# An attention and two-FFN kernel: 13 instead of 20 transfers per attention unit on SyncE's queue, x stored by GpSimd, the attention's order planned anew, six weight halves decoded after it

## The chip, the cores and the metric

The kernel runs on one core of one Trainium2 chip. The metric is the device time of one execution in microseconds. Before the change three runs gave 1263.87, 1264.07 and 1265.71 us (median 1264.07).

## What is computed

```python
B, H, S, D = 4, 8, 576, 64                                  # q, k, v: [B, H, S, D]
scores = q @ k.T / sqrt(D), causal;  a = softmax(scores);  local = a @ v
q_p = where(q > 0, q, exp(q) - 1) + 1
mem_out = (q_p @ M_prev) / (q_p . z_prev + 1e-6)            # M_prev [B,H,D,D], z_prev [B,H,D]
g = sigmoid(beta)                                            # one per head
x = g * mem_out + (1 - g) * local                            # -> [B*S = 2304, H*D = 512]
h = x @ w_in;  x = act(h) @ w_out                            # twice: 512 -> 2048 -> 512, own weights and act
```

Everything is float32; the weights come as float64, and the kernel decodes them itself from pairs of 32-bit words.

## The kernel before

**Attention, then the two FFN layers.** The attention is cut into 16 units u = 0 to 15, each one batch and one pair of heads. Layer 1 then runs over 18 chunks of 256 tokens in pairs, in two halves of the hidden width; layer 2 follows.

**One unit.** SyncE (SP in the rows) loads k, q and v (`load_rows`, three transfers each), for q two more (`qb`, the last 64 rows laid out apart for each head), and M_prev and z_prev (`load_mem`, four). TensorE (PE) transposes k and q into a PSUM tile (`k1`, `q1`); ScalarE (ACT) and VectorE (DVE) split them into two parts (`k2`, `k3`, `q2`, `q3`) and form q_p (`f1` to `f3`). PE makes the scores in four pieces (s0, s1, s2, s3; L478, L471); DVE masks and takes the row's extreme (L493), ACT the exponential (L497). PE transposes the exponentials (`ta`, `tb0` to `tb3`, L411), ACT moves them to SBUF (L506), and PE multiplies with v into the PSUM tile O: `v0` (L521), `v1`, `v2` (L528 to L531). `norms` (L537) puts q_p . z into O as well. DVE turns the sums into factors (`l1` to `l4`, L542 to L547), PE transposes them (`l5`, L548), ACT copies them out (`l6`, L550), and SP writes them to DRAM (`l7`, L551, r_d) and reads them back, repeated over the partitions, into tile R with three transfers (`l8`, `spread`, L560): two for the first plane of R, which weighs the local part, the third for the second plane. DVE multiplies O into R in two pieces (`weigh`, also x1, L575) and the memory's product (`m1`, L569, in a PSUM tile W) into R's second plane (x2, L578). GpSimd (POOL) adds the planes (x3, L580), and SP stores x (L581).

**What is shared.** There is one PSUM tile O, so `v0` of unit u+1 waits for `weigh` of unit u. There are three PSUM tiles W (W_101 to W_103 in the order's rows) for k1, q1, the scores, the transposes and m1; the tile of m1 comes free at x2. R has two buffers, but the plan gives every unit the same one, so the spread of u+1 also waits until x of u is stored.

**The order.** Every engine runs its instructions in a fixed order, which a planner writes (`Plan.order`): each step has an engine, a length, a priority (10 u + PRIO[key]), what it comes after and the buffers it needs; a lag is added to its end. A step on SP costs 80 to 330 ns per group of transfers, and the spread ends 2.5 us after its cost. The planner takes the step that can start first. The 16 halves of layer 1's first weights (`weight_half`: one 512 KB load into one of three buffers `raw`, two ACT and six DVE instructions each) and the first two token chunks (`first_chunk`) are steps of the same plan.

**Layer 1** starts with its own code order: per step of the hidden width 12 matmuls for h (L697 to L699), ACT and DVE for the activation (L707 to L713), and two steps later 12 matmuls for y (L727 to L729). Instructions of later weights are put between those of DVE (`fill`).

Of the kernel before, what the change touches and what calls it, by code (L numbers as in the profile page):

```python
# [9 lines left out]
F32R = mybir.dt.float32r  # L10
# [29 lines left out]
PRIO = dict(load=-14.0, k=-12.9, q=-8.2, phi=16.4, s0=-2.4, s1=0.8, s2=0.1, s3=0.6, ta=-9.1, tb0=4.7, tb1=4.8, tb2=-10.3, tb3=2.5,  # L40
            v0=8.6, n=34.3, l=7.5, v1=43.2, v2=11.8, m=11.9, x=38.4, w=(2.77, 1.99), c=10.2)
EVACUATE = dict(ta="ACT", tb0="ACT", tb1="ACT", tb2="ACT", tb3="ACT")
ROOMS = dict(W=3, O=1, q=2, k=2, v=2, mem=2, ks=2, qs=2, eq=1, ph=2, st=2, R=2, rt=2, e128=4, e256=4, e384=4, e512=4, e576=2,
# [18 lines left out]
class Plan:  # L62
# [25 lines left out]
    def order(self):  # L88
# [3 lines left out]
        while any(todo.values()):  # L92
            best = None
            for engine, ts in todo.items():
                first, now = None, idle.get(engine, 0.0)
                for t in ts:
                    x = self.ready(t, now)
                    if x is not None and (first is None or x < first[0] - 1e-9):
                        first = x, t
                        if x <= now + 1e-9:  # L100
                            break
# [3 lines left out]
            x, t = best  # L105
# [23 lines left out]
def attn_moe_moe_kernel(ctx, tc, q, k, v, m_prev, z_prev, beta, w1i, w1o, w2i, w2o, out):  # L129
# [71 lines left out]
    def new_e(w, i):  # L201
        x = att_tile(f"e{w}", i, w if w < S else 640)
        if w == S:
# [89 lines left out]
    def fetch_halves(seg, halves):  # L293
# [8 lines left out]
        raws = [load_raw(seg, *h) for h in halves[0:ahead]]  # L302
# [112 lines left out]
    stored = []  # L415

    def attention_unit(u):
# [5 lines left out]
        q, k, v, mem = Room("q"), Room("k"), Room("v"), Room("mem")  # L423
        ks, qs, eq, ph, st, R, O = Room("ks"), Room("qs"), Room("eq"), Room("ph"), Room("st"), Room("R"), Room("O")

        def load_q():
            x, qb = at(q)
            load_rows(q_in, x, u)
            for h in range(2):
                nc.sync.dma_start(out=qb[64 * h:64 * h + 64, h], in_=q_in[b, 2 * p + h, 512:576])  # L430

        def load_mem():
            m, z = at(mem)
            for h in range(2):
# [16 lines left out]
        q1 = add("PE", 670, "q", [ld_q], [t, q], lambda t=t: transposes(at(t), [  # L451
            (128 * j, at(q)[0][:, j].rearrange("p h d -> p (h d)")) for j in range(NKT)] + [
            (S, at(q)[1].rearrange("p h d -> p (h d)"))]), "T")
        q2 = add("ACT", from_psum(704), "q", [q1], [t, qs], lambda t=t: act.activation(
            at(qs)[:, 0], at(t)[:, 0:704], AF.Copy, scale=-0.125))
        q3 = add("DVE", dve(704), "q", [q2], [t, qs], lambda t=t: vec.scalar_tensor_tensor(
            out=at(qs)[:, 1], in0=at(t)[:, 0:704], scalar=-0.125, in1=as_r(at(qs)[:, 0]), op0=ALU.mult, op1=ALU.subtract))

        f1 = add("ACT", from_psum(S), "phi", [q1], [t, eq], lambda t=t: act.activation(at(eq), at(t)[:, 0:S], AF.Exp))
        f2 = add("DVE", 370, "phi", [f1], [eq], lambda: vec.tensor_scalar(  # L460
            out=at(eq), in0=at(eq), scalar1=1.0, scalar2=None, op0=ALU.min))
        f3 = add("DVE", dve(S), "phi", [f2], [t, eq, ph], lambda t=t: vec.scalar_tensor_tensor(
            out=at(ph)[:, 0:S], in0=at(t)[:, 0:S], scalar=0.0, in1=at(eq), op0=ALU.max, op1=ALU.add))
# [566 lines left out]
```

## Time and profile before

| | us |
|---|---|
| median of the three runs | 1264.07 |
| the profiled execution | 1263.82 |
| its span in the profile | 1262.0 |
| first spread of the attention (unit 0) issued at | 41.89 |
| last spread (unit 15) issued at | 451.88 |
| x2 of unit 15 starts at | 467.63 |

The 1.8 us between the span and the execution's own time lie around the program. Times in rows count from the span's start. A spread is found in the rows as three L560 transfers. A chain row gives start, length and what it was; a timeline row start, length, engine, line, operation, and in brackets the idle time ahead of it and what ended that.

### The profile page before, as it was taken

The page shows a single profiled execution, that of the slowest core. Times are in us where ns is not written, and L with a number is a line of the kernel's source. Part 1 is how long each engine was busy: PE and PEld are TensorE (multiplying, and loading weights), DVE is VectorE, ACT ScalarE, POOL GpSimd, SP SyncE. Part 2 cuts the span into 40 slices and gives each one's busy share as a digit, 9 for nine tenths or more (in the row PEclk, how much of TensorE's full clock was granted, in tenths as well). Part 3 has the DMA queues.
Part 4 walks back from the last instruction along what each step waited for, and adds up shares of the span by engine and source line. Part 5 has one row for each costly group of instructions (what it writes and reads, how often), then busy time and mean ns, then how long its engine had stood idle before and what let it go on. Part 6 is the DMA issues. An engine that isn't in the chain of part 4 may idle for free.

```text
span 1262.0 us, 18665 instructions
## 1 busy us (share of the span) xinstructions
PE 1083.3 (86%) x7032; PEld 954.5 (76%) x7032; DVE 770.9 (61%) x1706; ACT 516.4 (41%) x988; POOL 55.1 (4%) x59
## 2 busy tenths in 40 slices
PE   4767566667676559999999999999999999999998
PEld 3655445555454438888898887889999999999998
DVE  3554444545453314465985767669978789866665
ACT  3545433444453303243464233336444436443432
POOL 1000000000000000000000000000000000111121
PEclk9877676767677669999999999999999999999999
DMA  5333234333322112132441535422333311213121
GB/s 141 93 97 100 80 91 119 97 87 81 94 83 62 36 39 67 34 117 67 152 129 38 156 111 153 131 84 68 118 101 101 101 51 41 78 52 101 51 84 51
DMA packets 128858, 111.49 MB, mean 88 GB/s; under 512 B 73552, under 2 KB 108928, under 8 KB 128768
## 3 DMA queue, kind: packets, MB, share of 16 engines
q1 hardware_dynamic: 128480, 110.04, 29.3%
q8 instruction: 55, 0.90, 0.3%
q14 instruction: 35, 0.29, 0.1%
q10 hardware_dynamic: 288, 0.26, 0.1%
HBM read 86.52 MB, written 23.75 MB: 87 GB/s over the span
## 4 chain that ended last, share of the span: by engine, by line
PE 68%; DMA 21%; DVE 5%; SPq 3%; ACT 2%; issue 1%; DVEq 0%; ACTq 0%
DMA R<-r_d 19%; PE A L697 5%; PE A L698 5%; PE A L699 5%; PE A L770 5%; PE A L769 5%; PE A L768 5%; PE W L411 4%; PE y L793 2%; PE y L792 2%; PE y L791 2%; PE y L727 2%; PE y L728 2%; PE y L729 2%; PE W L478 2%; PE A L727 2%
## 5 line engine op out<-in xcount | busy, mean ns | idle before, releaser
L770 PE MATMUL A<-ffn_x,i 128*128 128x256 f32 x576 | 163.1, 283 | 0.0
L769 PE MATMUL A<-ffn_x,i 128*128 128x256 f32 x576 | 163.0, 283 | 0.0
L768 PE MATMUL A<-ffn_x,i 128*128 128x256 f32 x576 | 163.0, 283 | 0.0
L707 ACT ACTIVATE g<-A 128x512 f32<-128x512 f32 (+1 forms) x80 | 44.4, 555 | 258.3 <-PE A L699 258.2
L411 PE MATMUL W<-ident,e 128*128 128x128 f32 x400 | 82.8, 363 | 73.7 <-DVE R L578 51.9
L411 PEld LDWEIGHTS W<-ident,e 128*128 128x128 f32 x400 | 65.6, 195 | 83.3 <-DVE R L578 55.9
L965 ACT ACTIVATE gh<-g 128x896 fp32r<-128x896 f32 x72 | 68.8, 955 | 124.9 <-PE A L792 74.3
L709 DVE SCALAR_TENSOR_TENSOR g<-A,g 128x512 f32<-128x512 f32 (+1 forms) x80 | 50.8, 636 | 105.0 <-ACT g L708 105.0
L770 PEld LDWEIGHTS A<-ffn_x,i 128*128 128x128 f32 x576 | 110.6, 192 | 0.0
L768 PEld LDWEIGHTS A<-ffn_x,i 128*128 128x128 f32 x576 | 110.6, 192 | 0.0
L769 PEld LDWEIGHTS A<-ffn_x,i 128*128 128x128 f32 x576 | 110.6, 192 | 0.0
L944 DVE TENSOR_TENSOR gl<-g,gh 128x896 fp32r<-128x896 f32 x72 | 86.6, 1203 | 33.4 <-ACT gh L965 33.4
L493 DVE CUSTOM_DVE_ANT_0 e<-W,mask 128x128 f32<-128x128 f32 (+2 forms) x144 | 67.7, 517 | 34.5 <-PE W L478 22.6
L497 ACT ACTIVATE e<-e,mx 128x128 f32<-128x128 f32 (+2 forms) x144 | 82.4, 574 | 13.4 <-DVE mx L493 13.3
L506 ACT ACTIVATE pb<-W 128x640 f32<-128x640 f32 (+1 forms) x64 | 42.3, 674 | 98.2 <-PE W L411 97.8
L773 ACT ACTIVATE g<-A 128x512 f32<-128x512 f32 x72 | 42.8, 594 | 89.0 <-PE A L770 86.3
L521 PE MATMUL O<-pa,v 128*64 128x256 f32 (+1 forms) x128 | 22.1, 491 | 64.0 <-DVE R L575 64.0
L575 DVE TENSOR_TENSOR R<-O,R 128x256 f32<-128x256 f32 (+1 forms) x32 | 14.6, 458 | 101.0 <-DMA R<-r_d 98.7
L697 PE MATMUL A<-ffn_x,i 128*128 128x512 f32 (+1 forms) x160 | 60.1, 375 | 14.7 <-DVE R L578 14.7
L521 PEld LDWEIGHTS O<-pa,v 128*64 128x64 f32 x128 | 11.2, 197 | 73.1 <-DVE R L575 67.3
L578 DVE TENSOR_TENSOR R<-W,R 128x576 f32<-128x576 f32 x16 | 12.1, 757 | 82.1 <-DMA R<-r_d 82.1
L816 POOL TENSOR_TENSOR ys<-ys,pp 128x512 f32<-128x512 f32 x16 | 27.1, 1717 | 748.3 <-DVE ys L811 748.3
(210 smaller groups left out, 3119.8 us busy)
## 6 DMA issues: line engine op xcount, KB each, us to landing
raw<-in_moe_w_in_dram SPq DMA_DIRECT2D x32, 512.0 KB
raw<-in_moe_w_out_dram SPq DMA_DIRECT2D x32, 512.0 KB
xf<-y_d SPq DMA_DIRECT2D x18, 512.0 KB
xf<-x_d SPq DMA_DIRECT2D x10, 512.0 KB
R<-r_d SPq DMA_DIRECT2D x16, 288.0 KB
x_d<-R SPq DMA_DIRECT2D x16, 288.0 KB
xf<-yp_d SPq DMA_DIRECT2D x9, 512.0 KB
op_d<-ys SPq DMA_DIRECT2D x18, 256.0 KB
```

Source lines behind the costliest of these rows:

```text
L411: pe.transpose(t[:, c:c + 128], x, ident)
L493: lambda t=t, x=x, w=w, c=512 * h + c, mk=mk, col=col: vec.tensor_tensor_reduce(out=at(x)[:, 0:w], in0=at(t)[:, c:c + w], in1=mk, op0=ALU. ...
L497: lambda x=x, w=w, col=col: act.activation(at(x)[:, 0:w], at(x)[:, 0:w], AF.Exp, bias=at(st)[1][:, col:col + 1], scale=-1.0, accum_out=at( ...
L697: nc.tensor.matmul(hx, wh, xh[:, ct], start=(ct == 0), stop=False)
L698: nc.tensor.matmul(hx, wh, xl[:, ct], start=False, stop=False)
L699: nc.tensor.matmul(hx, wl, xh[:, ct], start=False, stop=(ct == 3))
L709: nc.vector.scalar_tensor_tensor(out=g, in0=hp, scalar=1.0, in1=g, op0=ALU.max, op1=ALU.min)
L768: nc.tensor.matmul(o, wh, xh[:, ct], start=(s == 0 and ct == 0), stop=False)
L769: nc.tensor.matmul(o, wh, xl[:, ct], start=False, stop=False)
L770: nc.tensor.matmul(o, wl, xh[:, ct], start=False, stop=(s == 1 and ct == 3))
L944: nc.vector.tensor_tensor(gl, g[:, 1:8], as_r(gh), ALU.subtract)
L965: nc.scalar.activation(gg[1], gg[0][:, 1:8], AF.Copy)
```

## The change

- The steps of a unit: q is loaded without `qb`, by three transfers; the last 64 rows are laid out apart by two GpSimd copies inside `qs` (`apart`, q4), and `q1`, `q2`, `q3` work on 576 columns instead of 704. q_p is built in its own tile `ph`.
- M_prev and z_prev are loaded once per batch (four transfers for four units) instead of per unit.
- x is stored by a transfer that GpSimd issues. q of unit 0 is loaded from ACT's queue.
- SP's steps now cost 570 ns per transfer (`SEND`) in the plan; the spread's lag stays 2.5 us. The priorities are new. The planner now prefers among ready steps the one with the lowest priority number, plus 1.25 (`STAY`) where PE would change its mode.
- The halves 10 to 15 of the weights are decoded in layer 1, at its steps 0 to 10; the first three of their loads stay in the plan.

```diff
+PRIO = dict(load=-48.26, v=-40.11, mem=-30.82, k=-3.3, q=-1.74, phi=35.91, s0=-19.51, s1=-15.79, ...
+EARLY, STAY = 10, 1.25
...
                 for t in ts:
+                    if first is not None and t.prio > first[2]:
+                        break
                     x = self.ready(t, now)
...
+                    if x > now + 1e-9:
+                        if first is None or x < first[0] - 1e-9:
+                            first = x, t, 1e9
+                    else:
+                        p = t.prio + STAY * (t.mode != mode and engine == "PE")
+                        if first is None or p < first[2]:
+                            first = now, t, p
...
-        def load_q():
-            x, qb = at(q)
-            load_rows(q_in, x, u)
-            for h in range(2):
-                nc.sync.dma_start(out=qb[64 * h:64 * h + 64, h], in_=q_in[b, 2 * p + h, 512:576])
...
+                r = slice(64 * h, 64 * h + 64)
+                nc.sync.dma_start(out=m[r, :, h], in_=m_prev[b, h::2].rearrange("p d e -> d p e"))
+                nc.sync.dma_start(out=z[r, :, h], in_=z_prev[b, h::2].rearrange("p d -> d p"))
+
+        if p == 0:
+            memory_of[b] = mem = Room("mem")
+            memory_of[b] = mem, add("SP", 2 * SEND + 2 * SEND, "mem", (), [mem], load_mem)
...
+        ld_k = add("SP", 3 * SEND, "load", (), [k], lambda: load_rows(k_in, at(k), u))
+        ld_q = add("SP" if u else "ACT", 3 * SEND, "load", (), [q], lambda: load_rows(q_in, at(q), u), lag=2.3)
+        ld_v = add("SP", 3 * SEND, "v", (), [v], lambda: load_rows(v_in, at(v), u))
...
+        def apart():
+            x = at(qs)
+            for h in range(2):
+                r = slice(64 * h, 64 * h + 64)
+                pool.tensor_copy(x[r, :, S + 64 * h:S + 64 * h + 64], x[r, :, 512:S])
+
+        q4 = add("POOL", 600, "q", [q3], [qs], apart)
...
-        l8 = add("SP", 240, "l", [l7], [R], spread, lag=2.5)
+        l8 = add("SP", 3 * SEND, "l", [l7], [R], spread, lag=2.5)
...
-        stored.append(add("SP", 80, "x", [x3], [R], lambda: nc.sync.dma_start(
+        stored.append(add("POOL", 1000, "x", [x3], [R], lambda: pool.dma_start(
             out=x_d[b][128 * p:128 * p + 128], in_=at(R)[:, 0])))
...
+    decoded = [weight_half(n, n // 2, n % 2) for n in range(EARLY)]
...
+    for h in late[0:RAWB]:
+        plan.add("SP", SEND, 10 * B * NP + 99, plan.tasks[-6:] + decoded, [Room("raw")], lambda h=h: first_raws.append(load_raw(0, *h)), lag=3.8)
+    for i, h in enumerate(late):
+        at_step(2 * i + 2, split_half, 0, *h)
+        for _ in range(5):
+            at_step(2 * i, piece, part)
```

PE's order from m1 of unit 9 to l5 of unit 10, before. O_104 is the PSUM tile O; rows of transposes that repeat are left out at "..." (`ident,e` is a transpose of exponentials, `ident,k` k1).

```order
L569 MATMUL W_101<-ph_136,mz_125 128x512
...
L411 MATMUL W_103<-ident,e_158 128x128
...
L521 MATMUL O_104<-pa_144,v_117 64x256 x2
...
L411 MATMUL W_101<-ident,e_162 128x128
...
L537 MATMUL O_104<-zz_122,ph_134 128x2 x5
...
L411 MATMUL W_103<-ident,k_113 128x128 x5
L478 MATMUL W_102<-ks_130,qs_132 128x128 x6
L478 MATMUL W_102<-ks_130,qs_132 128x256 x6
L478 MATMUL W_101<-ks_130,qs_132 128x512 x6
L548 MATMUL O_104<-ident,st_141 128x128
```

The same place with the change (line numbers are 8 to 13 higher).

```order
L582 MATMUL W_103<-ph_133,mz_117 128x512
...
L419 MATMUL W_101<-ident,e_155 128x128
...
L534 MATMUL O_104<-pa_141,v_113 64x256 x2
...
L550 MATMUL O_104<-zz_118,ph_131 128x2 x5
L419 MATMUL W_103<-ident,e_155 128x128
...
L419 MATMUL W_101<-ident,e_159 128x128
...
L491 MATMUL W_102<-ks_126,qs_127 128x128 x6
L491 MATMUL W_102<-ks_126,qs_127 128x256 x6
L561 MATMUL O_104<-ident,st_138 128x128
```

Before, tb3 into W_101, the tile that m1 of unit 9 holds until x2, stands ahead of norms, and k1 and s2 of other units stand ahead of l5. Now norms stands ahead of the first transposes into m1's tile (W_103), and between that point and l5 stand tb1, tb3 and s0 alone.

DVE's order from weigh of unit 9 to l4 of unit 10, before.

```order
L575 TENSOR_TENSOR R_146<-O_104,R_146 128x256
L575 TENSOR_TENSOR R_146<-O_104,R_146 128x320
L617 TENSOR_TENSOR w_1739<-da,dr 128x512
...
L578 TENSOR_TENSOR R_146<-W_101,R_146 128x576
L456 SCALAR_TENSOR_TENSOR qs_132<-W_102,qs_132 128x704
L460 TENSOR_SCALAR eq_133<-eq_133 128x576
L598 TENSOR_SCALAR da<-raw 128x512
L462 SCALAR_TENSOR_TENSOR ph_136<-W_102,eq_133 128x576
...
L544 TENSOR_SCALAR st_141<-O_104 128x10
...
L547 TENSOR_TENSOR st_141<-st_141,gates 128x19
```

With the change.

```order
L588 TENSOR_TENSOR R_143<-O_104,R_143 128x256
L588 TENSOR_TENSOR R_143<-O_104,R_143 128x320
L462 SCALAR_TENSOR_TENSOR qs_127<-W_102,qs_127 128x576
L591 TENSOR_TENSOR R_143<-W_103,R_143 128x576
L473 TENSOR_SCALAR ph_133<-ph_133 128x576
L475 SCALAR_TENSOR_TENSOR ph_133<-W_102,ph_133 128x576
L557 TENSOR_SCALAR st_138<-O_104 128x10
L559 RECIPROCAL st_138<-st_138 128x19
L560 TENSOR_TENSOR st_138<-st_138,gates 128x19
```

q3 has moved ahead of x2, and the decode's instructions (L598 to L617 before) no longer stand between.

SP's order between two spreads with the change: from the spread of unit 4 to that of unit 5.

```order
L573 DMA R_143<-r_d_175 128x1x576
L388 DMA q_105<-in_q_dram 128x4x64 x2
...
L388 DMA v_113<-in_v_dram 128x4x64 x2
...
L400 DMA raw<-x_d_187 128x4x256
L388 DMA k_111<-in_k_dram 128x4x64 x2
...
L286 DMA raw<-in_moe_w_in_dram 128x4x256
L564 DMA r_d_176<-rt_145 19x128
L289 DMA raw<-in_moe_w_out_dram 128x1024
L573 DMA R_143<-r_d_176 128x1x512
```

Here a load of weights stands between r_d and the spread; in units 9 to 14 nothing does, and the store of x is gone from this queue.

## Rows read from the trace of the kernel before

**Rows 1.** The page's head: span and instructions.
```profile
span 1262.0 us, 18665 instructions
```
**Rows 2.** Stretches: length, busy PE, PEld, DVE, ACT, POOL; granted clock, DMA share, GB/s.
```profile
42.00:468.00 426.00, 274.59 (x1759) 213.88 (x1759) 186.93 (x516) 174.87 (x427) 21.52 (x15) 0.71 0.30 82
468.00:520.00 52.00, 51.55 (x218) 42.51 (x219) 21.42 (x33) 15.25 (x29) 1.40 (x1) 0.95 0.20 63
462.00:467.00 5.00, 0.00 (x0) 0.00 (x0) 0.12 (x1) 0.00 (x0) 0.00 (x0) 0.50 0.13 51
```
**Rows 3.** The chain in order of time, spread of unit 8 to unit 9.
```profile
258.57 0.55 SPq L560
...
259.72 15.10 DMA R<-r_d
...
274.91 0.76 DVE R L578
...
275.82 2.37 PE W L411 x10
278.18 1.93 PE O L537 x10
280.11 2.23 PE W L411 x10
282.35 1.58 PE W L478 x7
283.92 0.42 PE O L548
...
284.71 1.60 DMA r_d<-rt
...
286.36 0.54 SPq L560
```
**Rows 4.** SP's timeline: spreads of units 0, 2, 6, 14, 15 and one r_d.
```profile
41.89 3.72 SPq L560 DMA_DIRECT2D R<-r_d  x3
...
89.17 0.26 SPq L551 DMA_DIRECT2D r_d<-rt  x1
93.64 4.92 SPq L560 DMA_DIRECT2D R<-r_d  x3
...
202.95 4.67 SPq L560 DMA_DIRECT2D R<-r_d  x3
...
424.21 3.75 SPq L560 DMA_DIRECT2D R<-r_d  x3
...
451.88 3.66 SPq L560 DMA_DIRECT2D R<-r_d  x3
```
**Rows 5.** DVE's timeline: x2 of unit 0, weigh's end and x2 of 15.
```profile
58.72 0.76 DVE L578 TENSOR_TENSOR R<-W,R 128x576 f32<-128x576 f32 x1 [3.96 <-DMA R<-r_d]
...
461.63 0.49 DVE L575 TENSOR_TENSOR R<-O,R 128x320 f32<-128x320 f32 x1 [1.97 <-DMA R<-r_d]
467.63 0.76 DVE L578 TENSOR_TENSOR R<-W,R 128x576 f32<-128x576 f32 x1 [5.51 <-DMA R<-r_d]
```
**Rows 6.** Timeline of the start: first scores of unit 0, and ACT's first decode.
```profile
14.03 1.30 PE L411 MATMUL W<-ident,k 128*128 128x128 f32 x5 [6.00 <-DMA k<-in_k_dram]
...
17.48 1.65 PE L478 MATMUL W<-ks,qs 64*128 64x128 f32 x12
...
23.98 0.68 ACT L593 ACTIVATE w<-raw 128x512 f32<-128x512 f32 x1 [5.64 <-DMA raw<-in_moe_w_in_dram]
```
**Rows 7.** Timeline at the attention's end: x3, store, and who waits for it.
```profile
468.52 1.40 POOL L580 TENSOR_TENSOR R<-R 128x576 f32<-128x576 f32 x1 [26.24 <-DVE R L578]
...
469.95 0.34 SPq L581 DMA_DIRECT2D x_d<-R  x1
...
472.15 0.69 DVE L713 TENSOR_TENSOR gl<-g,gh 128x512 fp32r<-128x512 f32 x1 [1.94 <-DMA x_d<-R]
```
**Rows 8.** DVE by line, 42 to 468 us: count, busy us, mean ns.
```profile
L617 DVE TENSOR_TENSOR w<-da,dr 128x512 f32<-128x512 f32 x15 | 10.8, 718 | 0.1
```

More of the change, by code (lines that the diff above doesn't have):

```diff
@@ L38 @@
 HALVES = {N1: [82 + 7 * i // 2 for i in range(16)], N1 + 1: [x for x in range(150, 209) if x % 8 in (0, 6)]}
-PRIO = dict(load=-14.0, k=-12.9, q=-8.2, phi=16.4, s0=-2.4, s1=0.8, s2=0.1, s3=0.6, ta=-9.1, tb0=4.7, tb1=4.8, tb2=-10.3, tb3=2.5,
-            v0=8.6, n=34.3, l=7.5, v1=43.2, v2=11.8, m=11.9, x=38.4, w=(2.77, 1.99), c=10.2)
+PRIO = dict(load=-48.26, v=-40.11, mem=-30.82, k=-3.3, q=-1.74, phi=35.91, s0=-19.51, s1=-15.79, s2=6.04, s3=-14.57, ta=-66.58, tb0=-44.92,
+            tb1=-21.43, tb2=-29.5, tb3=-16.11, v0=-23.74, n=-32.83, l=-36.92, v1=6.21, v2=23.96, m=23.51, x=55.42, w=(2.48, 4.3, 19.15), c=1.18)
+EARLY, STAY = 10, 1.25
 EVACUATE = dict(ta="ACT", tb0="ACT", tb1="ACT", tb2="ACT", tb3="ACT")
-ROOMS = dict(W=3, O=1, q=2, k=2, v=2, mem=2, ks=2, qs=2, eq=1, ph=2, st=2, R=2, rt=2, e128=4, e256=4, e384=4, e512=4, e576=2,
+ROOMS = dict(W=3, O=1, q=2, k=2, v=2, mem=2, ks=2, qs=2, ph=2, st=2, R=2, rt=2, e128=4, e256=4, e384=4, e512=4, e576=2,
              pa=2, pb0=1, pb1=1, pb2=1, pb3=1)
@@ L96, in order @@
                 for t in ts:
+                    if first is not None and t.prio > first[2]:
+                        break
                     x = self.ready(t, now)
[L98 to L101, printed above, removed]
+                    if x is None:
+                        continue
+                    if x > now + 1e-9:
[5 more added lines that the diff above has]
+                            first = now, t, p
                 if first is not None and (best is None or first[0] < best[0]):
@@ L301, in fetch_halves @@
             return
-        raws = [load_raw(seg, *h) for h in halves[0:ahead]]
+        raws = [load_raw(seg, *h) for h in halves[0:ahead]] if seg else first_raws
         for k, (f, x) in enumerate(halves):
@@ L376, in load_rows @@
     def load_rows(src, t, u):
+        queue = nc.scalar if u == 0 and src is q_in else nc.sync
         b, p = UNITS[u]
@@ L414, in attn_moe_moe_kernel @@
     WIDTH = (128, 256, 384, 512, S)
-    stored = []
+    stored, memory_of = [], {}
+    SEND = 570
     def attention_unit(u):
@@ L450, in attention_unit @@
         t = Room("W")
[L451 to L463, printed above, removed]
+        q1 = add("PE", 560, "q", [ld_q], [t, q], lambda t=t: transposes(at(t), [
+            (128 * j, at(q)[:, j].rearrange("p h d -> p (h d)")) for j in range(NKT)]), "T")
@@ L483, in attention_unit @@
             t = Room("W")
-            s = add("PE", cost, f"s{n}", [q2, q3, k2, k3], [t, qs, ks], lambda t=t, rows=rows: products(t, rows),
+            s = add("PE", cost, f"s{n}", [q3, k3, q4 if rows == (4,) else None], [t, qs, ks], lambda t=t, rows=rows: products(t, rows),
                     "T" if rows == (4,) else "R")
@@ L606, in high @@
             act.activation(got["o"][:, 0], got["w"], AF.Copy)
-        t = plan.add("SP", 80, prio - 20, (), [raw], load, lag=3.8)
+        t = plan.add("SP", SEND, prio - PRIO["w"][2], (), [raw], load, lag=3.8)
         t1 = plan.add("ACT", 574, prio, [t], [raw, w32], first)
@@ L619, in weight_half @@
         t2 = plan.add("ACT", 536, prio, [t2], [w32], high)
-        plan.add("DVE", 602, prio, [t2], [w32], low)
+        return plan.add("DVE", 602, prio, [t2], [w32], low)
     def first_chunk(i):
@@ L629, in load @@
             load_chunk(i, got["x"])
-        t = plan.add("SP", 80, prio, stored[0:NP], [raw], load, lag=3.8)
+        t = plan.add("SP", SEND, prio, stored[0:NP], [raw], load, lag=3.8)
         t = plan.add("ACT", from_sbuf(1024), prio, [t], [raw], lambda: act.activation(ffn_x[0][:, i], got["x"], AF.Copy))
@@ L981, in attn_moe_moe_kernel @@
         attention_unit(u)
-    for n in range(2 * NSLOT):
-        weight_half(n, n // 2, n % 2)
+    decoded = [weight_half(n, n // 2, n % 2) for n in range(EARLY)]
     for i in range(2):
         first_chunk(i)
+    late = sorted(((n // 2, n % 2) for n in range(EARLY, 2 * NSLOT)), key=lambda h: (h[1], h[0]))
+    first_raws = []
+    part = fetch_halves(0, late)
+    for h in late[0:RAWB]:
[4 more added lines that the diff above has]
+            at_step(2 * i, piece, part)
     engines = {e.engine for e in (nc.tensor, nc.scalar, nc.vector, nc.gpsimd)}
```

47 lines of the change are left out of this document (25 added, 22 removed).

## The prediction

> **What bounds the kernel now.** I read stretches first, then the chain in order of time over one unit, then SP's and DVE's timelines. The span is 1262.0 us [rows 1]; the execution took 1263.8, 1.8 more, and lies 0.3 under the median of 1264.07, so differences are taken from 1263.8 and stand for the median as well. The stretches show that from 42 to 468 us PE is busy 275 of 426 us at a mean granted clock of 0.71, DVE 187 and ACT 175, so no engine is full; from 468 on PE has no gap (51.6 of 52 us) [rows 2]. The attention is therefore bound by a wait, the later layers by PE, and what the change is worth is decided before 468 us.
>
> The wait is seen in one unit [rows 3]. The spread of unit 8 is issued at 258.57, its third transfer lands before x2 at 274.91, x2 ends at 275.67, and the spread of unit 9 is issued at 286.36. So a unit's cycle has two parts: from spread to the end of x2, 17.1 us (17.6 in unit 0, 16.5 in unit 15 with no loads beside it [rows 4, 5]), and from there to the next spread, 10.7 us, which I call the tail. Spread 0 is at 41.89, spread 15 at 451.88: 410.0 us for 15 cycles, 27.3 each [rows 4]. The cycle closes because weigh frees O for v0 of the next unit and x2 frees m1's tile W, on which transposes ahead of l5 wait.
>
> **The spread itself stays.** Its three transfers are unchanged. While only they run, DMA is busy 0.13 of 16 engines, two engines' worth, at 51 GB/s [rows 2]: the 576 KB are limited by themselves, not by the queue's other transfers. I take 17.4 us per unit from spread to x2's end, and 16.5 in units 14 and 15. Taking 7 transfers per unit off SP gives nothing by itself: the chain of rows 3 has SP only for the spread's own issue.
>
> **The tail, step by step.** In rows 3 it is 0.15 us to PE, ten transposes 2.37, norms 1.93, ten more 2.23 (tb1 and k1), scores 1.58, l5 0.42, then 0.37 over l6 to the issue of r_d and 1.65 until the spread: 10.7. In the new order of unit 9 to 10 norms stands ahead of the tile that waits for x2, and weigh is done early enough for it: weigh's second piece starts 9.8 us after the spread in unit 15 and takes 0.5 [rows 4, 5], v0 I put at 1.6 like the scores, tb2 at 1.2 (half of 2.37), norms at 1.93, together 15.0 us after the spread, before x2's end. What is left behind x2 on PE is tb1 (1.2), tb3 (four of five, 0.95), s0 (1.58), l5 (0.42), with 0.15 ahead and 0.37 behind 4.7; with 1.65 the tail is 6.3. DVE's part behind x2 (f2, f3, l2 to l4: five instructions, none wider than x2 with its 0.76 [rows 5], so at most 3.8, an estimate) lies beside tb1, tb3 and s0 (3.9 with the 0.15). Cycle: 17.4 + 6.3 = 23.7.
>
> I went through the other units in the same way, by what stands on PE behind the tile freed by x2, and on SP between r_d and the spread:
> - Units 9 to 13 are alike: 5 x 23.7 = 118.5. Unit 8 has one weight load between r_d and the spread, tail 7.3: 24.7. Unit 6 has tb2, ta and l5 behind x2: tail 5.85, 23.3. Unit 7 has tb1, norms, tb3, s0, l5: tail 8.7, 26.1. Unit 14 has tb3, norms, v1, l5: 16.5 + 7.7 = 24.2. Sum for units 6 to 14: 216.8, where before they took 451.88 - 202.95 = 248.9 [rows 4]: **-32.1**.
> - Units 0 to 5 are worse placed. In unit 1 x2 stands ahead of weigh on DVE, so v0, tb1, norms, tb3, s0, s1, v1 and l5 all follow x2 (13 us), and a weight load and three k transfers stand between r_d and the spread. Such a row of loads made r_d to spread 4.5 us in unit 1 before (89.17 to 93.64 [rows 4]); tail 17.2. Unit 0 has two weight loads just ahead of r_d (10.5), unit 3 the load of the first token chunk, which waits for the store of unit 3 (10.3), unit 4 a load between r_d and spread that waits for DVE (8.6), unit 5 norms behind x2 (11.1), unit 2 8.2. Tails 65.9, and 6 x 17.4 = 104.4: 170.3 against 202.95 - 41.89 = 161.1: **+9.2**.
> - The start. Before, PE makes the first scores at 17.48, because k1 of unit 1, whose data came at 14.03, and q1 behind it stand ahead; and ACT stands 5.6 us until 23.98 at a decode that waits for its load [rows 6], with the exponentials behind it. Now the scores follow q1 and no decode is ahead. I take 7 us for the first (from 17.48 to 10.5; bounds 3 and 9) and 5.6 for the second: r_d, before about 40.3 (41.89 less 1.6), comes at 27.7. But a weight load and four memory transfers now stand between r_d and the spread on SP, five at 0.55 or somewhat more [rows 3] beyond r_d's own 0.3, and the load lies ahead of the spread in the engines; so spread 0 comes at about 31.3: **-10.6**, with bounds of 28 and 37.
> - Layer 1. Six halves of six DVE instructions, 0.72 each [rows 8], so 4.3 us per half, are put into its first six steps, beside three of 0.69 [rows 7]: 6.4 us of DVE at most against 24 matmuls of 0.24 on PE (51.55 for 218 [rows 2]), 5.7 us a step. Six steps run 4.2 us behind at most, and y comes two steps, 11 us, after its h: hidden. If that cover goes, because gl of the first step also waits for the store of unit 15 [rows 7], up to 6 us come onto the path; bounds 0 and 6, I take **+1.0**, nearer to the row without a gap.
>
> Edits at nothing: 704 to 576 columns in q2 and q3, one transpose fewer, fewer memory transfers, ten halves instead of sixteen on DVE and ACT inside the attention. All lie in DVE's and PE's waits for the spread; they cost or give nothing as long as the spread lasts longer than that work. `apart` on GpSimd stands ahead of x3 of the unit before and is needed by s3 only after l5.
>
> **The store by GpSimd** changes a wait. All units use the same buffer R, so the spread of unit u+1 waits on SP for the store of unit u, now on another engine's transfer. Before: x3 ends about 1.5 us after x2, SP issues at once, and the store is in before 472.15 (issued 469.95, so 2.2 us) [rows 7]: 3.7 us after x2. GpSimd's transfers are in no row; I put its landing 1 us later, 4.7 us after x2, 1.6 us before the regular spread at 6.3, so it costs nothing. Bounds: as soon as SP's (3.7), or after the DVE work that follows x2 (x2 + 10). The Trainium skill speaks against this edit: "SBUF — State Buffer", section "SBUF: two separate sides", says that while DVE runs certain SBUF-to-SBUF operations GpSimd can't write the descriptors of its transfers, and that they then seem blocked. No row here shows a transfer from GpSimd, and this stands below as a rival. By "DMA: Bandwidth & Descriptors", section "Anatomy of one DMA — SWDGE (gpsimd) path", such a transfer of 295 KB takes 2.0 us and 0.7 for its bytes, an estimate of 2.7 from that page, by which the landing would be at x2 + 4.2 and the sum the same.
>
> **Sum.** -10.6 + 9.2 - 32.1 + 1.0 = -32.5; 1263.8 - 32.5 = 1231.3, rounded to 1231.
>
> **Rivals.**
> 1. PE or the store come a little late in the regular units. From l5 to v0 PE has s3, s1, v1, ta, k1, s2, v2, q1, m1 and tb0, ten groups of 1.2 to 1.6 us as in rows 3, so 12 to 16, begun 2.5 us ahead of the spread; if v0 comes at spread + 13 instead of 10.8, norms ends after x2 and each of nine units loses about 2 us; a store at x2 + 8.5 costs about the same (2.2 in each of units 9 to 13, less in four others: 16). Then 1247 (1242 to 1258). For it: mean clock 0.71, and a plan that thinks the spread is in 2.5 us after its issue. Against: PE's 275 us are 17 us per unit [rows 2] in a cycle of 23.7.
> 2. The new order gains nothing where it counts: it is planned for a spread of 2.5 us, which takes 15 us; if the early units lose 20 instead of 9 and the regular tails are 8.5, the sum is -10.6 + 20 - 13 + 1: 1261, the same. For it: unit 1 shows that the planner puts v1 ahead of l5. Against: the rows of five equal units.
> 3. Slower: GpSimd's store holds R. If it lands L us after x2, each unit loses L minus its tail where that is positive: for L = 10 some 32 us, all of the gain; so it decides from about 10 us after x2, 8.5 after x3, four times SP's 2.2. At L = 12 it costs 58: 1289. For it: f2, f3 and l2 to l4 run on DVE just when GpSimd prepares the store, and the two may hold each other up (the page named above says so). Against: those are short, 0.76 us or less each.
> 4. Faster than forecast: units 0 to 5 as quick as before (0 instead of +9.2): 1222.
>
> **Chances.** Forecast (1221 to 1242) 0.60, rival 1 0.18, rival 2 0.06, rival 3 0.08, rival 4 and below 0.08. Range 8 in 10: 1218 to 1253; it holds the forecast, most of rival 4 and half of rival 1. A measurement of this kernel tells 0.2% (2.5 us) from no change. Faster 0.86 (forecast, rivals 1 and 4), same 0.06, slower 0.08.
>
> **What would show it.** In the changed profile: first spread near 31; units 9 to 13 with 23 to 24.5 us between spreads and norms ahead of x2's end; unit 1 the longest cycle, near 35; last x2 near 434; no gap on PE in the first 50 us of layer 1. I am wrong if regular spreads wait for x's store (GpSimd's transfer landing later than 6 us after x2), if v0 there starts later than 13 us after the spread, or if the first spread is still near 42.

## The result and the profile after

The changed kernel takes 1222.86 us (four runs, 1221.88 to 1225.75), the kernel before, beside it, 1264.57 (four runs, 1263.87 to 1265.71): a ratio of 0.9673, 95% interval 0.9655 to 0.9691. The forecast was 1231, in a range of 1218 to 1253. The profiled execution has a span of 1220.8 us, 41.2 less than [rows 1].

The stretches after, columns as in [rows 2]:

```profile
28.00:407.00 379.00, 265.20 (x1738) 205.82 (x1735) 169.79 (x483) 169.37 (x418) 41.13 (x58) 0.73 0.31 86
427.00:467.00 40.00, 34.78 (x146) 26.42 (x145) 30.09 (x54) 16.31 (x27) 0.00 (x0) 1.00 0.37 113
467.00:520.00 53.00, 53.00 (x236) 43.88 (x235) 29.10 (x50) 19.83 (x40) 0.00 (x0) 1.00 0.29 87
```

The attention is still bound by a wait (PE busy 265 of 379 us, clock 0.73), only shorter. New is the second line: PE has 5.2 us of gaps in the first 40 us of layer 1, where before it had 0.4 in 52.

The chain of waits in a regular unit (11 to 12) answers to [rows 3]:

```profile
311.45 14.76 DMA R<-r_d
...
326.30 0.77 DVE R L591
...
327.12 2.18 PE W L419 x9
329.30 1.58 PE W L491 x8
330.87 0.41 PE O L561
```

Behind x2 (L591) stand nine transposes (2.18), scores (1.58) and l5 (0.41). Norms and ten transposes, 4.2 us in [rows 3], are no longer between; norms run ahead of x2.

SP's timeline, answering to [rows 4]: r_d (L564) and spread (L573) of unit 0, spreads of units 6, 14 and 15.

```profile
24.52 0.32 SPq L564 DMA_DIRECT2D r_d<-rt  x1
28.08 3.78 SPq L573 DMA_DIRECT2D R<-r_d  x3
...
191.37 3.93 SPq L573 DMA_DIRECT2D R<-r_d  x3
...
379.48 4.25 SPq L573 DMA_DIRECT2D R<-r_d  x3
406.86 3.65 SPq L573 DMA_DIRECT2D R<-r_d  x3
```

The start, answering to [rows 6] (PE's timeline), and the end of the attention, answering to [rows 7] (chain):

```profile
9.44 0.69 PE L491 MATMUL W<-ks,qs 64*128 64x128 f32 x4 [0.74 <-ACT qs L460]
```
```profile
422.59 0.77 DVE R L591
...
423.44 1.41 POOL R L593
...
425.13 2.39 DMA x_d<-R
```

GpSimd issues the store 0.29 us after x3, and it lands 2.39 us later, at x2 + 4.2.

In the table are the stretches of each profiled execution, worked out from its spreads on SP and its x2 on DVE; "rest" is from x2's end in unit 15 to the end of the span. The time is the median of the runs; a row's stretches come from one of them, which for e9 was 5.4 us above its median and for c1, e8 and e11 3.7 to 4.4 below. e9 has the changed kernel's attention, in the same order, and still ends its last x2 4.6 us later, so stretches ahead of it that differ by that much tell nothing by themselves. "Rest" is steadier: 797.0 to 797.7 in seven of the eight rows with the changed kernel's layer 1 (e8 has 802.8, not traced). The last two are combinations; the rest are told in the order of the questions.

| kernel | spread 0 at | units 0-5 | units 6-14 | x2(15) ends | rest | time us | ratio to before, interval |
|---|---|---|---|---|---|---|---|
| before | 41.89 | 161.1 | 248.9 | 468.4 | 793.6 | 1264.57 | 1 |
| changed | 28.08 | 163.3 | 215.5 | 423.4 | 797.5 | 1222.86 | 0.9673 (0.9655-0.9691) |
| e3 old order | 40.13 | 173.6 | 244.0 | 474.2 | 797.7 | 1273.74 | 1.0079 (1.0064-1.0094) |
| e10 seven behind spread | 29.02 | 170.9 | 220.3 | 436.9 | 797.5 | 1237.99 | 0.9795 (0.9780-0.9809) |
| e2 seven behind q | 44.23 | 179.8 | 225.3 | 465.8 | 797.4 | 1264.58 | 0.9995 (0.9980-1.0009) |
| e1 store on SyncE | 28.06 | 166.1 | 215.2 | 425.9 | 797.0 | 1224.78 | 0.9693 (0.9678-0.9707) |
| e6 sixteen halves early | 28.93 | 165.2 | 228.6 | 439.2 | 792.5 | 1231.77 | 0.9746 (0.9729-0.9763) |
| e9 late pieces spread out | 29.00 | 166.4 | 216.1 | 428.0 | 790.5 | 1214.90 | 0.9617 (0.9594-0.9640) |
| e8 planned with 15 us | 26.98 | 193.0 | 248.2 | 484.6 | 802.8 | 1293.18 | 1.0233 (1.0216-1.0251) |
| e11 two places swapped | 27.11 | 161.2 | 215.0 | 419.7 | 797.5 | 1222.71 | 0.9678 (0.9662-0.9694) |
| e5 before, quick spread | 42.38 | 107.2 | 158.2 | 314.8 | 793.7 | 1109.80 | 0.8774 (0.8747-0.8801) |
| e4 changed, quick spread | 27.93 | 104.0 | 129.6 | 268.7 | 797.5 | 1068.97 | 0.8471 (0.8445-0.8497) |
| c1 = e4 + e9 | 29.03 | 102.9 | 126.3 | 265.4 | 790.5 | 1062.01 | 0.8396 (0.8377-0.8415) |
| c2 = c1, SyncE kept free | 26.01 | 102.8 | 131.2 | 267.0 | 790.5 | 1060.73 | 0.8395 (0.8378-0.8411) |

### The profile page after: what moved, and what is told of

It reads as the page before. It is cut to its first block, busy times and chain, and to the rows that moved or that the text cites. A ratio compares the mean times of both kernels' runs of the same rounds, so it can differ in the third digit from the quotient of the medians.

```text
span 1220.8 us, 18534 instructions
## 1 busy us (share of the span) xinstructions
PE 1072.3 (88%) x7016; PEld 944.2 (77%) x7016; DVE 769.9 (63%) x1708; ACT 515.2 (42%) x988; POOL 76.9 (6%) x105
## 4 chain that ended last, share of the span: by engine, by line
PE 67%; DMA 21%; DVE 7%; ACT 2%; issue 2%; SPq 1%; POOL 0%; DVEq 0%; ACTq 0%
DMA R<-r_d 19%; PE A L783 5%; PE A L782 5%; PE A L781 5%; PE A L711 5%; PE A L712 5%; PE A L710 5%; PE W L419 3%; PE y L806 3%; PE y L805 2%; PE y L804 2%; PE W L491 2%; PE y L740 2%; PE y L741 2%; PE y L742 2%
## 5 line engine op out<-in xcount | busy, mean ns | idle before, releaser
L720 ACT ACTIVATE g<-A 128x512 f32<-128x512 f32 (+1 forms) x80 | 44.3, 554 | 217.9 <-PE A L712 215.6
L419 PE MATMUL W<-ident,e 128*128 128x128 f32 x400 | 78.6, 353 | 65.5 <-DVE R L591 57.1
L419 PEld LDWEIGHTS W<-ident,e 128*128 128x128 f32 x400 | 62.0, 186 | 78.3 <-DVE R L591 60.0
L722 DVE SCALAR_TENSOR_TENSOR g<-A,g 128x512 f32<-128x512 f32 (+1 forms) x80 | 50.8, 635 | 96.5 <-ACT g L721 96.4
L957 DVE TENSOR_TENSOR gl<-g,gh 128x896 fp32r<-128x896 f32 x72 | 86.6, 1203 | 33.4 <-ACT gh L978 33.4
L519 ACT ACTIVATE pb<-W 128x640 f32<-128x640 f32 x64 | 42.9, 675 | 147.2 <-PE W L419 147.0
L506 DVE CUSTOM_DVE_ANT_0 e<-W,mask 128x128 f32<-128x128 f32 (+3 forms) x144 | 67.7, 517 | 56.5 <-PE W L491 47.4
L510 ACT ACTIVATE e<-e,mx 128x128 f32<-128x128 f32 (+3 forms) x144 | 82.5, 574 | 18.7 <-DVE mx L506 18.5
L591 DVE TENSOR_TENSOR R<-W,R 128x576 f32<-128x576 f32 x16 | 12.1, 757 | 94.1 <-DMA R<-r_d 94.1
L710 PE MATMUL A<-ffn_x,i 128*128 128x512 f32 (+1 forms) x160 | 59.8, 374 | 11.1 <-DVE R L591 11.1
L711 PE MATMUL A<-xl,i 128*128 128x512 f32 (+1 forms) x160 | 59.0, 369 | 0.6 <-DVE xl L683 0.6
L711 PE MATMUL A<-ffn_x,i 128*128 128x512 f32 (+1 forms) x160 | 59.4, 371 | 0.0
```

Of the source, the lines that this page charges most:

```text
L419: pe.transpose(t[:, c:c + 128], x, ident)
L506: lambda t=t, x=x, w=w, c=512 * h + c, mk=mk, col=col: vec.tensor_tensor_reduce(out=at(x)[:, 0:w], in0=at(t)[:, c:c + w], in1=mk, op0=ALU. ...
L510: lambda x=x, w=w, col=col: act.activation(at(x)[:, 0:w], at(x)[:, 0:w], AF.Exp, bias=at(st)[1][:, col:col + 1], scale=-1.0, accum_out=at( ...
L710: nc.tensor.matmul(hx, wh, xh[:, ct], start=(ct == 0), stop=False)
L711: nc.tensor.matmul(hx, wh, xl[:, ct], start=False, stop=False)
L722: nc.vector.scalar_tensor_tensor(out=g, in0=hp, scalar=1.0, in1=g, op0=ALU.max, op1=ALU.min)
```

## Experiments: is it the order?

**e3: the changed kernel, planned by the rule, priorities and sending costs of before.**

```diff
-PRIO = dict(load=-48.26, v=-40.11, ...
+PRIO = dict(load=-14.0, v=-14.0, mem=-14.0, k=-12.9, ...
...
-            x, t = best[0:2]
+            x, t = best
...
-        ld_k = add("SP", 3 * SEND, ...
+        ld_k = add("SP", 200, ...
...
```

> The changed kernel with the order planned as in the kernel before: its rule of choice, its priorities, its short costs of sending (0.08 to 0.33 us). Transfers, store on GpSimd, columns, q of unit 0 on ScalarE and late halves stay as changed. My theory (the order alone brings the gain of units 6 to 14): units 6 to 14 take 245 us or more together again, and the time is 1245 to 1260 us. Rival (fewer and smaller transfers and a shorter q path bring it, the order adds little): below 1232 us.

1273.74 us: slower than before and above my range; units 6 to 14 take 244.0, just under the 245 I had set. Its chain from unit 8 to 9:

```profile
258.23 0.77 DVE R L584
...
259.13 2.37 PE W L412 x10
261.50 1.93 PE O L543 x10
263.42 2.23 PE W L412 x10
265.66 1.43 PE W L484 x9
267.09 0.26 PE O L554
```

That is [rows 3] again, step for step. The fewer transfers, the narrower q and the ten halves take nothing off this tail, and the first spread is at 40.13. Without the new order nothing of the gain is there. Rule, priorities and sending costs went back together, so the share of each is not shown.

## Experiments: do SyncE's transfers matter?

**e10 and e2: seven small transfers per unit put back, behind each spread (e10) or behind q's loads (e2).** Every engine keeps the order of the changed kernel; the plan does not know of the seven.

```diff
...
+            x = at(more)
+            for h in range(2):
+                r = slice(64 * h, 64 * h + 64)
+                nc.sync.dma_start(out=x[r, 0], in_=q_in[b, 2 * p + h, 512:576])
+                nc.sync.dma_start(out=x[r, 1 + h], in_=m_prev[b, 2 * p + h])
+                nc.sync.dma_start(out=x[r, 3, h:h + 1], in_=z_prev[b, 2 * p + h].unsqueeze(1))
+            nc.sync.dma_start(out=x[0:64, 4], in_=q_in[b, 2 * p, 512:576])
...
```

> The changed kernel with the same seven extra transfers per unit on SyncE's queue as in the run that added them behind the loads of q, but here straight behind each spread, so that none comes at the start or between an r_d and its spread; they delay only the loads behind them, by 4 us. What is left of my statement that fewer transfers give nothing by themselves: 1223 to 1228 us. Rival (the number of transfers on the queue itself costs, wherever they stand): 1240 to 1263 us, most of it in units 0 to 8, where weight loads fill the queue.

> The changed kernel with seven more transfers per unit on SyncE's queue, put behind the loads of q: the sizes and sources of those that were taken away (64x64 pieces of q and of the memory, and 64x1 columns), written into a tile that nobody reads. SyncE has 20 transfers per unit again, in the changed order. My theory (taking transfers off SyncE gives nothing by itself): 1223 to 1226 us, the three microseconds only if a group of seven, some 4 us of issuing, falls between an r_d and its spread. Rival (SyncE's issuing time is part of the path, seven times 0.55 us in each of 16 units): 1240 to 1280 us.

e10 takes 1237.99, e2 1264.58: put behind q's loads, the seven take the whole gain; behind the spreads, 15.1 us of it. In e2 16.2 us of it are the start. There l5 of unit 0 ends at 26.22 us, 3.0 later than in the changed kernel, but r_d is issued only at 40.07 (SP's timeline), behind 28 of the added transfers:

```profile
40.07 0.43 SPq L574 DMA_DIRECT2D r_d<-rt  x1
```

In e10 the cycles of units 10 to 14 sum to 120.3 us against 120.1: there my statement holds. Until the last x2 13.6 us are lost, in other units: 3.2 of them in the tail of unit 7, 11.5 instead of 8.3 us. SP there, in the changed kernel and then in e10:

```profile
219.18 4.03 SPq L388 DMA_DIRECT2D k<-in_k_dram  x2
223.31 3.33 SPq L389 DMA_DIRECT2D k<-in_k_dram  x1
...
234.88 0.64 SPq L286 DMA_DIRECT2D raw<-in_moe_w_in_dram  x1
238.04 0.26 SPq L564 DMA_DIRECT2D r_d<-rt  x1
239.77 4.35 SPq L573 DMA_DIRECT2D R<-r_d  x3
```
```profile
226.86 3.48 SPq L577 DMA_DIRECT2D more<-in_q_dram  x1
...
246.61 0.61 SPq L286 DMA_DIRECT2D raw<-in_moe_w_in_dram  x1
247.33 0.30 SPq L564 DMA_DIRECT2D r_d<-rt  x1
250.72 4.05 SPq L573 DMA_DIRECT2D R<-r_d  x3
```

The first issues behind a spread take 4.03 for two and 3.33 and 3.48 for one, where elsewhere one takes 0.6. The first three issues behind a spread (units 0 to 13) are through 5.5 to 9.0 us after it in the changed kernel, and what is behind slides towards the next r_d. In e10 l5 ends at 245.46 (chain), but r_d is issued only at 247.33, right behind a weight load; in the changed kernel it is issued 0.3 us after l5's end. That load is then on its way beside r_d, and r_d to spread takes 3.4 instead of 1.7. The number of transfers counts where the queue is full: in units with weight loads or the memory's four transfers. A plan that counts the seven was not tried, so what 20 transfers cost in an order made for them is open.

**e1: the store back on SyncE, at its planned place.**

```diff
-        stored.append(add("POOL", 1000, "x", [x3], [R], lambda: pool.dma_start(
+        stored.append(add("POOL", 1000, "x", [x3], [R], lambda: nc.sync.dma_start(
...
```

> The changed kernel with one edit: x's store is issued by SyncE instead of GpSimd, at the same place of the planned order. My theory (the store on GpSimd costs and gains nothing, because the spread of the next unit comes later than the store's landing): 1223 us, within 2.5 of the changed kernel's 1222.9. Rival A (part of the gain comes from SyncE no longer standing at the store with loads and r_d behind it): 1228 to 1245, with r_d or loads in SyncE's queue behind a wait for x3. Rival B (GpSimd's transfer is the slower one and holds the next spread): 1217 or less.

1224.78, 1.9 above the changed kernel, within the 2.5 of my theory; the intervals overlap. The profile has 2.5 us more until the last x2, all in units 0 to 5, which is less than two executions of one attention differ by. Who issues the store hardly matters, and rivals A and B fall.

## Experiments: the late halves

**e6: all sixteen halves in the attention.**

```diff
-EARLY, STAY = 10, 1.25
+EARLY, STAY = 16, 1.25
```

> The changed kernel with all sixteen weight halves decoded in the attention, as before, none in the first steps of layer 1. My theory: the late halves are what layer 1 loses, 3.8 us from x2 of unit 15 to the end, and six halves more in the attention lie in waits for the spread, but for a load or two between an r_d and its spread: 1219 to 1224 us, with no gap of PE behind the attention. Rival (the decode and its loads do hold the attention up): 1230 to 1245 us, with the loss in units 8 to 14, where the six halves would go.

1231.77: the rival. My part on layer 1 held (rest 792.5 instead of 797.5, 5.0 less), but x2 of unit 15 ends 15.8 us later, 13.1 of it in units 6 to 14. Weight loads stand in SP's queue again, and the order is planned differently: in unit 8's tail, 10.2 us instead of 6.4, the chain has norms and more transposes and scores behind x2. What is the load's share and what the order's, this run does not separate.

**e9: the late pieces spread over fifteen half-steps.**

```diff
-    late = sorted(((n // 2, n % 2) for n in range(EARLY, 2 * NSLOT)), key=lambda h: (h[1], h[0]))
+    late = sorted(((n // 2, n % 2) for n in range(EARLY, 2 * NSLOT)), key=lambda h: (h[0] + 2 * h[1], h))
...
-        at_step(2 * i + 2, split_half, 0, *h)
-        for _ in range(5):
-            at_step(2 * i, piece, part)
+        for k in range(5):
+            at_step((5 * i + k) // 2, piece, part)
+        at_step((5 * i + 4) // 4 * 2 + 2, split_half, 0, *h)
```

> The changed kernel with the thirty decoding pieces of the six late halves spread over fifteen half-steps of layer 1 instead of six steps of five, in the order in which the halves are used; their ScalarE part comes one step behind. My theory (VectorE at 6.4 to 6.8 us a step against PE's 5.5 is what layer 1 loses): with 5.5 us a step or less PE has no gap, 4 to 5 us less from the last x2 to the end, 1218 us, 1216 to 1220. Rival (the loss is the wait of the first step for x's store and the chunk's load, whatever is decoded): 1222 to 1224.

1214.90, ratio 0.9617 (0.9594 to 0.9640), below the changed kernel's interval. The rest falls by 7.0 us, more than expected. 40 us from the same place of layer 1 on, PE has no gap:

```profile
432.00:472.00 40.00, 40.00 (x177) 32.87 (x176) 33.01 (x59) 16.57 (x28) 0.00 (x0) 1.00 0.44 132
```

What held PE was not that DVE is full: it is busy 30.1 of 40 us in the changed kernel and 33.0 here. The changed kernel's chain shows a loop of two engines:

```profile
428.22 0.69 DVE w L254
...
428.94 0.63 ACT i L335
429.57 0.49 ACT g L720
...
430.09 0.64 ACT g L721
...
430.75 0.69 DVE g L722
...
435.01 0.70 DVE w L254
435.73 0.63 ACT i L335
```

ACT's split of a half (L335) waits for the last decoding piece on DVE (L254), the activation of the step (L720, L721) stands behind it on ACT, and DVE's g (L722), with the next pieces behind it, waits for that: 6.8 us a turn, against 24 matmuls of 0.23, 5.5 us, on PE. PE's matmuls for y wait six times for DVE's gl (L726), 4.6 us in all from 427 to 467 us; in e9 none does. e9 takes the wait away, thins the pieces and uses the halves in another order at once, and does not tell these apart.

## Experiments: the planner's odd places

**e8: the plan is told of a spread of 15 us.**

```diff
-        l8 = add("SP", 3 * SEND, "l", [l7], [R], spread, lag=2.5)
+        l8 = add("SP", 3 * SEND, "l", [l7], [R], spread, lag=15.0)
```

> The changed kernel planned with 15 us from the issue of a spread to its landing instead of 2.5, no other number changed. My theory (the planner's wrong length puts v1 ahead of l5 in unit 14 and x2 ahead of weigh in unit 1, 4 and 8 us lost): unit 14's cycle falls from 27.4 to 23.5 and unit 1's from 32.5 to 25, 1205 to 1216 us. Rival (the priorities were found for 2.5 us, and the order with 15 is worse in the regular units): 1228 to 1260 us.

1293.18: my theory fell. Nearly every tail is now 11.6 us. The chain behind x2 is five transposes, norms, v1 (L541 to L544), l5, v2: with the true length the planner puts v1 ahead of l5 in the regular units too. That this is because the priorities suit 2.5 us is not shown. Another 23 us go in units 0 and 1, where spread to x2's end takes 31.5 and 26.7 us and the chain runs through weight loads and their decoding. Only unit 14's cycle falls as I thought, to 21.7 us: there v1 and v2 both stand ahead of l5, and l6 starts 0.1 us behind l5.

**e11: in unit 15 v1 and v2 behind l5, in unit 1 x2 behind weigh.**

```diff
...
+        mark[u] = l5, v1, v2, x1, x2
...
+        done = plan.order()
+        l5, v1, v2 = mark[15][0:3]
+        for t in (v2, v1):
+            if done.index(t) < done.index(l5):
+                done.remove(t)
+                done.insert(done.index(l5) + 1, t)
+        x1, x2 = mark[1][3:5]
+        done.remove(x2)
+        done.insert(done.index(x1) + 1, x2)
...
```

> The changed kernel with its planned order altered at two places by hand: in unit 15 PE's v1 is put behind l5 instead of ahead of it, and in unit 1 VectorE's x2 behind weigh instead of ahead of it. Nothing else is moved. My theory (a unit's tail is set by what stands on PE and VectorE between the tile that x2 frees and l5): the cycle from unit 14 to 15 falls from 27.4 to 23 to 24.2, that from unit 1 to 2 from 32.5 to 25 to 27, together 9 to 11 us: 1212 to 1215 us. Rival (the planner's two odd places cost nothing; something else, such as SyncE's loads in unit 1 and l4's late reciprocal in unit 15, ends there): 1220 to 1224.

1222.71: no change that the runs can tell. In the profile, which is of the fastest of the four (1219.02), unit 1's cycle falls by 3.8, to 28.7, unit 14's only by 0.6, to 26.8. There l5 now starts 3.9 us behind x2 instead of 6.2, and it does not matter (chain of e11):

```profile
396.78 0.48 PE O L561
...
401.10 0.03 PE O L542
...
401.20 0.28 ACT rt L563
```

l5 (L561) ends at 397.26; ACT copies its result (l6, L563) only at 401.20, released by v2's last matmul (L542). l5 and v2 write different columns of the one tile O, and l6 stands behind v2 in the program, so its wait counts v2 in. I had moved v1 behind l5 without moving l6 ahead of both. Moving l6 too was not tried.

## Experiments: the spread itself

**e4 and e5: the spread in six transfers of 64 partitions, in the changed kernel and in the kernel before.**

```diff
...
-            for x, c0, c1, src in ((0, 0, 512, rows(0, 512, 512)), ...
-                nc.sync.dma_start(out=at(R)[:, x, c0:c1], in_=src)
+            for x, c0, c1, at0, step in ((0, 0, 512, 0, 512), (0, 512, S, 1024, 64), (1, 0, S, 1152, 640)):
+                for h in range(2):
+                    src = flat[at0 + step * h:at0 + step * h + c1 - c0].unsqueeze(0).broadcast_to([64, c1 - c0])
+                    nc.sync.dma_start(out=at(R)[64 * h:64 * h + 64, x, c0:c1], in_=src)
```

> The changed kernel with each of the three transfers of a spread written as two, 64 partitions each, so that the source's outermost dimension has 64 steps instead of 2. Same bytes, six transfers instead of three, order as changed. My theory (the spread runs on two of the 16 DMA engines and this sets the unit's cycle): DMA share beside a lone spread rises from 0.13 to 0.5 or more, the transfer takes 3 to 6 us instead of 15, and the cycle falls from 23.4 to about 18 us, where PE's work of 17 us per unit is the bound: 1223 - 15 x 5 = 1150 us, 1135 to 1180. Rival A (the 576 KB are limited by something else, such as the read of one DRAM row by many): the spread keeps 14 to 15 us and the time is 1222 to 1235 with three more issues per unit. Rival B (the spread is fast, but PE's wait for other things takes its place): 1180 to 1210.

> The kernel before with each transfer of a spread written as two of 64 partitions, nothing else. My theory (a spread that lands in 3 to 4 us instead of 15 takes up to 11.5 us off each cycle, until PE's 17 us a unit or SyncE's 20 transfers decide): 1264 - 16 x 9.5 = 1110, 1080 to 1150 us; the change's own worth with a quick spread is the difference to 1069, some 40 us as with the slow one. Rival (what the change wins is only a tail behind a slow spread): within 5 us of 1069, the change is worth nothing any more.

e4 takes 1068.97 us, 154 less than the changed kernel, e5 1109.80. The chain of e4 at unit 15 and its stretches:

```profile
264.58 3.27 DMA R<-r_d
```
```profile
28.00:260.00 232.00, 210.98 (x1733) 162.39 (x1730) 168.13 (x483) 167.09 (x418) 41.10 (x58) 0.96 0.53 141
195.00:260.00 65.00, 63.96 (x555) 49.35 (x554) 39.77 (x127) 46.62 (x118) 12.48 (x18) 1.00 0.37 105
```

A spread's transfer lands in 2.4 to 4.4 us in the rows of the chain, here 3.27, where the last one took 14.5 to 15.8 in the changed kernel. The DMA share beside a lone spread, 0.40 (263.2 to 265.2 us), is three times the old one, but not the 0.5 I expected. From 195 us on PE is busy 64.0 of 65, at the upper clock level (1.00, 2.4 GHz), and a unit takes 13.4 us (units 10 to 13; the mean of all cycles is 15.6). My 1150 was too slow because I put PE's work at 17 us a unit; that was its busy time at a mean clock of 0.71. With the waits gone the granted clock is 1.00, and the same norms take 1.01 us instead of 1.93:

```profile
226.17 0.86 PE O L534 x8
...
227.73 1.01 PE O L550 x10
228.74 1.04 PE W L419 x9
229.78 0.89 PE W L491 x12
230.67 0.26 PE O L561
```

The chain there is PE alone. The queue behind the spread is free, too: in e4 two pieces of v are issued in 0.92 us right behind it, and the first three issues are through in 1.7 to 2.6 us instead of 5.5 to 9.0.

The Trainium skill has the rule: "DMA: Bandwidth & Descriptors", section "Rules for kernel authors", says that the slowest dimension of the access patterns sets how many engines a transfer uses, and that a leading dimension of c < 16 confines it to c. The old source leads with 2, and [rows 2] show 0.13 of 16 engines; the trace agrees.

The change's worth is the same beside a quick spread: e4 to e5 is 0.8471 / 0.8774 = 0.9655, 40.8 us, as expected. Its gain is not only a tail behind a slow spread.

**c1: e4 and e9 together; c2: c1 with SyncE kept free in the plan from r_d to the spread.** The edits of c1 are those above. That of c2:

```diff
-        l7 = add("SP", 300, ..., lag=2.4)
+        l7 = add("SP", 2300, ..., lag=0.0)
```

> Both edits that the runs point to: the spread in six transfers of 64 partitions, and the late pieces spread over layer 1. If their gains add, 1069 - 4.5 = 1064.5, 1062 to 1067 us. Rival (with the quicker attention layer 1 begins at another state of the loads, and the pieces wait for raw halves instead): 1067 to 1072.

> As the run with both edits, but the plan keeps SyncE free from an r_d to its spread (r_d's task costs 2.3 us and lands at once), so that no load is issued between the two. My theory (in units 0, 1, 4, 5, 8 and 9 of the run with the quick spread 3 to 5 us instead of 1.7 stood between them, 13 us together, and the chain of waits goes through it): 1050 to 1058 us. Rival (those loads come later then, and VectorE's decoding, which fills the early units, waits for them; or the whole order comes out otherwise): 1062 to 1085 us.

c1 takes 1062.01: the gains add (1068.97 less e9's 8.0 is 1061.0). c2 takes 1060.73, the same. No load stands between r_d and spread any more, yet in eight units 2.4 to 5.2 us still pass. SP's timeline of c2:

```profile
174.53 0.25 SPq L564 DMA_DIRECT2D r_d<-rt  x1
176.25 3.67 SPq L572 DMA_DIRECT2D R<-r_d  x6
...
201.76 0.61 SPq L289 DMA_DIRECT2D raw<-in_moe_w_out_dram  x1
202.46 0.30 SPq L564 DMA_DIRECT2D r_d<-rt  x1
206.87 3.67 SPq L572 DMA_DIRECT2D R<-r_d  x6
```

SP waits for r_d's landing: 1.7 us from issue to issue where the queue is clear, 4.4 right behind a 512 KB weight load. In seven of the eight units such a load (once of tokens) was issued 0.7 to 2.4 us ahead of r_d, in the eighth pieces of q; in unit 1, the 5.2, the store of unit 0 landed 1.0 us after r_d and held the spread on. So a load that is on its way delays r_d, whether or not one is issued behind it, and my theory fell; the cycles went up and down with other moves of the plan. c1 and c2 are the fastest here, 16% below the kernel before.

## Why the prediction came out as it did

The sum by its own steps, from the spans: start -13.8 (forecast -10.6), units 0 to 5 +2.2 (+9.2), units 6 to 14 -33.4 (-32.1), layer 1 and after +3.8 (+1.0): -41.2 instead of -32.5.

- **The bound.** Right, and larger than I made of it: spread to x2's end stayed at 17.0 us (17.4 taken), and e4 shows what it held back. I read 0.13 of 16 engines in [rows 2] and wrote that the transfers "are limited by themselves", which is true, and did not ask what in their form does it.
- **Units 9 to 13.** 116.3 us (118.5), tails 6.1 to 6.4 (6.3). e3 supports the cause: with the old order the norms and ten transposes are back behind x2.
- **Unit 14.** 27.4 instead of 24.2. I had v1 ahead of l5; the copy l6 waits for v2 as well, as e11 shows: r_d comes 2.5 us after l5's end there, 0.4 in a regular unit.
- **Units 0 to 5.** Mis-sized: tails 60.3 instead of 65.9 (unit 1 15.3 for 17.2, units 4 and 5 2.9 less together), spread to x2's end 103.0 for 104.4. Unit 1 was the longest, 32.5 instead of 35, and e11's swap took 3.8 off it.
- **The start.** Scores came 8.0 us earlier (7 taken), r_d at 24.52 (27.7 taken); from r_d to the spread 3.6 as worked out. The old order alone puts the spread back to 40.13. Of the 3.2 us that I missed 1.0 lie ahead of the scores and 2.1 between scores and r_d (15.1 us; 22.8 before). What SP's emptier queue is worth ahead of r_d is not in this step; e2 shows that it matters there.
- **Layer 1.** This step failed: "Six steps run 4.2 us behind at most [...]: hidden". It counted DVE's busy time and left out that ACT's activation stands behind a split which waits for DVE. The loop took 6.8 us a step, and 3.8 us came onto the path, inside the bounds of 0 and 6.
- **Edits at nothing.** Wrong as a statement: "Taking 7 transfers per unit off SP gives nothing by itself" holds for units 10 to 14 (e10); over all the seven cost 15 us there, and in e2, by their place, the whole gain. Halves put back cost 8.9 in all (e6). The sum was spared because the tails were read from the new order, with its emptier queue, unit by unit. The converse half was right: by e3 these edits alone gain nothing.
- **The store.** Right as a price, wrong as "costs nothing" everywhere. It landed 2.4 to 2.6 us after its issue in eleven units, in unit 15 at x2 + 4.2 (4.7 taken), but 3.0 to 5.2 us after it in units 0, 2, 3, 4 and 8, and that of unit 4, 7.2 us after x2, held the next spread by 0.3 us (chain):

```profile
159.48 5.20 DMA x_d<-R
...
164.75 0.53 SPq L573
```

Rival 3 fell. The blocking that the Trainium skill's "SBUF — State Buffer", section "SBUF: two separate sides", describes shows in no row: in unit 6 DVE is busy for the 1.2 us behind the issue and the store lands in 2.39 us, in unit 8 DVE is idle there and it takes 3.84. SyncE's stores in e1 are the slow ones in units 0, 2, 4 and 8 as well (4.4 to 4.9, else 2.1 to 2.5). The estimate from the Trainium skill's "DMA: Bandwidth & Descriptors", section "Anatomy of one DMA — SWDGE (gpsimd) path", was 2.7 us; 2.39 were measured in unit 15.
- **Rivals 1 and 2** fell: v0 starts 10.4 us after the spread in unit 10's cycle (286.80, 297.16), and the regular tails were as worked out. Rival 4's 1222 is the time that came, but by its mechanism only in part: units 0 to 5 lost 2.2, and the start gave 3.2 more.

What stays open: which part of the planning (rule, priorities, sending costs) brings the order's gain; how e6's loss divides between loads and order, and e9's gain between wait and thinning; and unit 14 with l6 moved too.

## What to carry to other kernels

Ask of every transfer on the path not only how long it takes but how many DMA engines it runs on: 0.13 of 16 beside a lone transfer was worth 154 us, nearly four times this change. Two parts of a change can need each other: the emptier queue without the order gained nothing (e3), and the order without the emptier queue kept 27 us or nothing, by where the added transfers stood (e10, e2). So a part costed "at nothing" must be costed in both orders. Where ACT and DVE feed each other within a step, follow the loop once around; busy shares of 0.75 do not show it.

## What the runs showed of the hardware

A transfer that moves at two DMA engines' worth (0.13 of 16) also held up the queue that issued it: the first three issues behind it were through in 5.5 to 9.0 us, and in 1.7 to 2.6 once the spread went in transfers of 64 partitions. A weight load of 512 KB ahead of the 10 KB of r_d made the time from r_d to the spread 4.4 us instead of 1.7. And PE's granted clock rose from a mean of 0.73 to 0.96 in the attention as its waits went, with nothing else changed than the spread, so that the bound worked out from its busy time was a quarter too high (17 us a unit against 13.4).
